# Denominators of the last attention pass from matmuls with ones, read in PSUM

## The chip, the cores and the metric

The kernel runs on one core of a Trainium2 chip. The metric is the device time of one execution in microseconds (us): the median of seven runs before the change is 894.89 us (894.72 to 896.04). One further execution was recorded by the hardware profiler; all durations below come from it. Its engines are TensorE (PE for matmuls, PEld for weight loads), VectorE (DVE), ScalarE (ACT), GpSimd (POOL) and SyncE (SP, which issues the DMAs here). Matmul results go to PSUM, which has eight banks of 512 fp32 columns; everything else on the chip is kept in SBUF.

## The reference

Two identical transformer layers over 2048 tokens of width 448, with the same weights: attention with 16 heads of 28 columns, and a feed-forward part of width 1792 with a squared ReLU. Cut to what matters:

```
def _A_ref(x, wqkv, wo):
    qkv = (x @ wqkv).reshape(B, S, 3, H, Dh)      # H = 16, Dh = 28
    scores = einsum("bhqd,bhkd->bhqk", q, k) * Dh ** -0.5
    p = softmax(scores, axis=-1)
    o = einsum("bhqk,bhkd->bhqd", p, v)
    return o.reshape(B, S, D) @ wo
def _B_ref(x, w1, b1, w2, b2):
    h = maximum(x @ w1 + b1, 0)
    return (h * h) @ w2 + b2
for _ in range(2):
    x = x + _A_ref(_layernorm(x), A_wqkv, A_wo)
    x = x + _B_ref(_layernorm(x), B_w1, B_b1, B_w2, B_b2)
return x
```

## The kernel before

**Tiles and passes.** Tokens lie in 16 tiles of 128 (`tb` 0 to 15). Heads are padded from 28 to 32 rows and worked on four at a time, a head group `g` of 0 to 3, so one group fills the 128 partitions with four strips `hh` of 32. Queries are cut into blocks `qb`: of two tiles, but of one tile each for the last two blocks of layer 1 (tile 14 and tile 15). A pass is one block and one head group over all keys. The last pass of the list (`end`, number 115) is layer 1, tile 15, head group 3; the last four passes are the four head groups of tile 15.

**Scores, exponentials, products.** `s_stream` writes scores in groups of three units of 512 columns into one of two three-bank PSUM buffers (`sc`, L809); a unit is one head strip, so consecutive matmuls sit in different 32-row strips of TensorE. To keep TensorE busy it may write the same scores again (`again`, L800), if its own clock says that there is room. ScalarE takes the exponential of each group (`pt`, L834); a few units are exponentiated on VectorE instead. `p_stream` multiplies the probabilities with the values (L982): the matmuls of one pass accumulate into one bank `oT`, each head in a column strip of 32 (`tile_position=(0, 32*hh)`), in the order strip 0, 1, 2, 3, 0, 1, ... V is padded with ones in its columns 28 to 31, so the rows 28 to 31 of each strip of `oT` hold the sum of the probabilities: the softmax denominator. In a pass of tile 15 there are 64 such matmuls of 128 columns, in four steps of 16 (one step for every four key tiles `kb`); a step of the last pass is issued as soon as its exponentials exist.

**Normalising.** When a pass is done, VectorE copies `oT` to `oT_sb` in SBUF (L1005). For most blocks the denominators go through DRAM and are inverted there in pairs (`norm_pair`). For tile 15 `norm_stream` does it on the engines: a fp32 matmul with the selection matrix `sel` spreads each head's denominator over its 32 rows in a bank `den` (L1047), VectorE inverts that bank (L1053) and multiplies (L1058) into `oTn`.

**What follows.** `chain` then runs for each block: the product with `wo` (L553 `wo,oTn`, four matmuls, one per head group; for tile 15 each waits for its own group), the sum with x on VectorE (L1113), the statistics (L448, L449), the inverse root on GpSimd (L470, L471), the normalisation (L520), transposes on TensorE (L493), their copy (L505), 14 slices of `w1` with four matmuls of 128 columns each (56, L553 `w,xnT`), ReLU (L1158 on ScalarE, L1160 on VectorE), square (L1165, L1167), the product with `w2` (one matmul for the bias and 14 more, 448 columns; for tile 15 in two parts of 320 and 128 columns, `HALF`), the sum with x and the store of the tile (L1188, on SP's queue).

**What sets the order.** Nothing is scheduled by hand or by a compiler: `Planner` runs all these streams against a cost model of its own and emits each engine's instructions in that order. Each operation names what it depends on, what buffer it acquires and what it releases. A PSUM bank (`bank`) comes from two single-bank pools (the page calls tiles there `mt`, `oT`, `den`, `tp`) and, once all scores are issued (`s_left` empty, token `"send"`), also from the two score buffers, whose tiles the page then calls `sc`. A matmul tile holds its bank until VectorE or ScalarE has read it.

Of the kernel before, what the change touches and what calls it, by code (L numbers as in the profile page):

```python
# [11 lines left out]
DT = mybir.dt  # L12
AF = mybir.ActivationFunctionType
ALU = mybir.AluOpType
P = 128
H = 16
DH = 28
DHP = 32
G = 4
QB = 512  # L20
QR = 256
# [196 lines left out]
def kernel(  # L218
# [12 lines left out]
    nc = tc.nc  # L231
# [29 lines left out]
    pl = Planner()  # L261
# [144 lines left out]
    def bank(o, name):  # L406

        if o.res in R_m:
            return ps_m[R_m.index(o.res)].tile([P, 512], DT.float32, name=name, tag="m")[:, :]
        return ps_sc.tile([P, 3 * 512], DT.float32, name="sc", tag="sc")[:, 0:512]  # L410
# [260 lines left out]
    for pi, (l, qb, g, kbs, first, last) in enumerate(passes):  # L671
        r = 4 // blocks[l][qb][1]
# [259 lines left out]
    def p_stream():  # L932


        for pi, (l, qb, g, kbs, first, last) in enumerate(passes):
            nt = blocks[l][qb][1]
            r, n = 4 // nt, nt * P
            todo = list(kbs[::r])
            end = pi == len(passes) - 1
            some = 1 if end else CHUNK  # L940
            hold = todo[0 if end else min((HOLD if nt == 2 else HOLD1) * len(todo) // 8, len(todo) - 1)]
            box = {}
            p_next[0] = next(i for i, u in enumerate(units) if u[0] == pi and u[1] == hold) + G - 1

            def done(kb):

                return ("u", pi, kb) in pl.tok and all(("x" if k == 3 else "e", gi) in pl.tok for gi, k, _ in where[pi, kb])

            def got(kb):

                yield Op("-", 0.0, None, deps=[("u", pi, kb)])
                yield Op("-", 0.0, None, deps=[("e", gi) for gi, k, _ in where[pi, kb] if k < 3])
            yield from got(hold)
            while todo:
                now = [kb for kb in todo if done(kb)][:some]
                if len(now) < min(some, len(todo)):
                    kb = next(kb for kb in todo if not done(kb))
                    if ("u", pi, kb) not in pl.tok or any(k < 3 and ("e", gi) not in pl.tok for gi, k, _ in where[pi, kb]):
                        yield from got(kb)
                        continue  # L960
                    if (e_now[1] - min(gi for gi, _, _ in where[pi, kb]) < NPT - KEEP and e_now[1] < len(gbuf) - 1
                            and len(todo) > len(now) + 1):
                        yield Op("-", 0.0, None, deps=[("e", e_now[1] + 1)])
                        continue

                    now = sorted(now[:some - 1] + [kb])
                    yield Op("-", 0.0, None, deps=[("x", gi) for gi, k, _ in where[pi, kb] if k == 3])
                todo = [kb for kb in todo if kb not in now]
                begin, close = "t" not in box, not todo

                def fn(e, now=now, begin=begin, close=close, box=box, pi=pi, l=l, g=g, r=r, n=n):
                    if "t" not in box:
                        p_next[0] = None
                        box["t"] = bank(box["o"], "oT")
                    held[0] -= sum(k == 3 for kb in now for _, k, _ in where[pi, kb])
                    for kb in now:
                        for i in range(r):
                            for gi, k, hh in where[pi, kb]:
                                p, c0 = gbuf[gi]["pt"], k * 512 + i * n
                                if k == 3:  # L980
                                    p, c0 = gbuf[gi]["pd"], i * n
                                nc.tensor.matmul(box["t"][DHP * hh:DHP * hh + DHP, 0:n],  # L982
                                                 lhsT=V_sb[l][:, kb + i, 4 * g + hh, :],
                                                 rhs=p[:, c0:c0 + n],
                                                 start=begin and kb == now[0] and i == 0,
                                                 stop=close and kb == now[-1] and i == r - 1,
                                                 tile_position=(0, DHP * hh))
                by = [(("x" if k == 3 else "e"), gi) for kb in now for gi, k, _ in where[pi, kb]]
                o = Op("PE", 0.02 + 0.22 * len(now), fn,
                       deps=[*by, *{("V", l, kb + i) for kb in now for i in range(r)}],  # L990
                       acq=None if "o" in box else pools_now(),
                       rel=[gbuf[gi][w] for w, gi in by], mode="col")
                box.setdefault("o", o)
                yield o
            res = {}
            def ev(e, box=box, first=first, last=last, g=g, res=res, n=n, l=l, qb=qb):
                pair = pairs.get((l, qb, g // 2))
                src = box["t"][:, 0:n]
                if last:
                    dst = res["t"] = pair["t"][:, g % 2, :]  # L1000
                    dst = dst[:, 0:n]
                else:
                    dst = part(l, qb, g)
                if first:
                    nc.vector.tensor_copy(out=dst, in_=src)  # L1005
                else:
                    nc.vector.tensor_tensor(out=dst, in0=src, in1=part(l, qb, g), op=ALU.add)
            if last and (l, qb, g // 2) not in pairs:
                def both(e, l=l, qb=qb, g=g):
                    pairs[l, qb, g // 2]["t"] = osp.tile([P, 2, QR], DT.float32, name="oT_sb")  # L1010
                pairs[l, qb, g // 2] = {"own": Op("DVE", 0.0, both, acq=R_os), "ev": [], "res": []}
                yield pairs[l, qb, g // 2]["own"]
            pair = pairs[l, qb, g // 2] if last else None
            oe = Op("DVE", 0.15 + n / 930, ev, deps=[o], rel=box["o"])
            yield oe
            if last:
                pair["ev"].append(oe)
                pair["res"].append((g, res))
                if qb == len(blocks[l]) - 1:
                    pl.spawn(3, norm_stream(l, qb, g, res, oe, pair))  # L1020
                elif len(pair["ev"]) == 2:
                    pl.spawn(3, norm_pair(l, qb, g - g % 2, pair))

    def norm_start(l, qb):
        if (l, qb) not in oTn_of:
            def take(e):
                oTn_of[l, qb][0] = np_.tile([P, G, QR], DT.bfloat16, name="oTn")
            oTn_of[l, qb] = [None, Op("DVE", 0.0, take, acq=R_on)]
            yield oTn_of[l, qb][1]

    def norm_end(l, qb, m, gs):

        norm_done.setdefault((l, qb), []).extend([m] * gs)
        if len(norm_done[l, qb]) == G - ((l, qb) == (1, len(blocks[1]) - 1)):
            pl.spawn(LASTP if (l, qb) == (1, len(blocks[1]) - 1) else NLP + 0.1 * (qb - len(blocks[1])) if l == 1 and qb >= len(blocks[1]) - NL else 4 + 0.1 * qb, chain(l, qb))

    def norm_stream(l, qb, g, res, oe, pair):


        t0, nt = blocks[l][qb]  # L1040
        n = nt * P
        box = {}
        yield from norm_start(l, qb)

        def den(e):
            box["t"] = bank(d, "den")
            nc.tensor.matmul(box["t"][:, 0:n], lhsT=sel[:, :], rhs=res["t"][:, 0:n], start=True, stop=True)  # L1047
        d = Op("PE", 0.1 + n * 4 / 2400, den, deps=[oe], acq=pools_now())
        yield d

        def rcp(e):
            box["r"] = rp.tile([P, 2, QR], DT.float32, name="rec")[:, 0, :]
            nc.vector.reciprocal(out=box["r"][:, 0:n], in_=box["t"][:, 0:n])  # L1053
        r = Op("DVE", n * 0.0066, rcp, deps=[d], rel=d, acq=R_rec)
        yield r

        def mul(e):
            nc.vector.tensor_tensor(out=oTn_of[l, qb][0][:, g, 0:n], in0=res["t"][:, 0:n],  # L1058
                                    in1=box["r"][:, 0:n], op=ALU.mult)
        m = Op("DVE", 0.13 + n / 930, mul, deps=[r, oTn_of[l, qb][1]], sets=("on", l, qb, g))  # L1060
        yield m
        yield Op("DVE", 0.0, None, deps=[m], rel=r)
        pair.setdefault("mul", []).append(m)
        if len(pair["mul"]) == 2:
            yield Op("DVE", 0.0, None, deps=[m], rel=pair["own"])
        norm_end(l, qb, m, 1)

    def norm_pair(l, qb, g, pair):
# [200 lines left out]
```

The softmax here doesn't subtract the row's maximum and nothing guards it: scores larger than these inputs give would overflow.

## Time and profile before

| what | value |
|---|---|
| median of 7 runs | 894.89 us (894.72 to 896.04) |
| the profiled execution | 894.89 us |
| its span, first to last instruction | 893.1 us |
| busy: PE / DVE / ACT | 831.1 (93%) / 794.1 (89%) / 878.7 us (98%) |
| the exponentials (L834) | 683, 863.8 us |
| end of the last exponential | 877.07 us |
| last sum with x on VectorE | 890.49 to 890.78 us |
| granted TensorE clock | 1.00 in every stretch from 867.5 us to the end |

The 1.8 us between the time and the span lie outside of what the profiler records of the instructions. The page says of each group of instructions how long it was busy and what its engine waited for. The chain of waits follows the work that ended last back to the start. A timeline row is `start, duration, engine, line, operation, out<-in, shape, count`. A row of several matmuls lasts from the start of the first to the end of the last, and since they are pipelined, the step from one to the next is shorter than the duration of one: the 64 products of a pass of tile 15 last 1.08 us, and one alone some 0.22 us.

From its start to about 870 us the chain is the stream of exponentials on ScalarE. The change concerns the 23 us after that: the last pass, the normalisation of tile 15 and the feed-forward part of the tiles 14 and 15, of which the attention half of tile 14 is already done.

### The profile page before, as it was taken

The page shows a single profiled execution, that of the slowest core. Times are in us where ns is not written, and L with a number is a line of the kernel's source. Part 1 is how long each engine was busy: PE and PEld are TensorE (multiplying, and loading weights), DVE is VectorE, ACT ScalarE, POOL GpSimd, SP SyncE. Part 2 cuts the span into 40 slices and gives each one's busy share as a digit, 9 for nine tenths or more (in the row PEclk, how much of TensorE's full clock was granted, in tenths as well). Part 3 has the DMA queues.
Part 4 walks back from the last instruction along what each step waited for, and adds up shares of the span by engine and source line. Part 5 has one row for each costly group of instructions (what it writes and reads, how often), then busy time and mean ns, then how long its engine had stood idle before and what let it go on. Part 6 is the DMA issues. An engine that isn't in the chain of part 4 may idle for free.

```text
span 893.1 us, 29098 instructions
## 1 busy us (share of the span) xinstructions
PE 831.1 (93%) x12829; PEld 458.5 (51%) x12829; DVE 794.1 (89%) x1572; ACT 878.7 (98%) x707; POOL 38.9 (4%) x98
## 2 busy tenths in 40 slices
PE   8999999998999999999989998888999999999998
PEld 4555654554545545454554554444544544545566
DVE  7988999999889999999989999899898999989654
ACT  8999999999999999999999999999999999999995
POOL 3100000000000000100000000001000000000000
PEclk9999999999999999999999999999999999999999
DMA  9100100000000000000000000011000000000100
GB/s 263 37 3 3 27 18 11 14 14 15 14 2 15 15 14 14 13 10 7 2 2 2 2 2 2 3 39 39 10 18 19 20 25 19 20 8 19 32 14 18
DMA packets 33915, 18.43 MB, mean 21 GB/s; under 512 B 18874, under 2 KB 33339, under 8 KB 33788
## 3 DMA queue, kind: packets, MB, share of 16 engines
q1 hardware_dynamic: 33788, 16.58, 6.6%
q8 instruction: 100, 1.64, 0.8%
q14 instruction: 27, 0.22, 0.1%
HBM read 14.26 MB, written 2.07 MB: 18 GB/s over the span
## 4 chain that ended last, share of the span: by engine, by line
ACT 68%; issue 12%; PE 10%; DVE 6%; DMA 2%; SPq 1%; POOL 0%; DVEq 0%
ACT pt L834 68%; PE mt L553 3%; PE sc L809 3%; PE oT L982 2%; DVE v_h L909 1%; DVE K_sb L909 1%; DMA dn<-oT_sb 1%; DMA rec<-scr 1%; DVE r L1160 1%; PE sc L553 1%; DVE st L448 1%; DVE oTn L1104 0%; SPq L303 0%; DMA x_sb<-in_A_x_dram 0%; DVE v_e L904 0%
## 5 line engine op out<-in xcount | busy, mean ns | idle before, releaser
L834 ACT ACTIVATE pt<-sc 128x1536 bf16<-128x1536 f32 (+1 forms) x683 | 863.8, 1569 | 1.8 <-PE sc L809 1.4
L809 PE MATMUL sc<-Q_sb,K_sb 32*128 32x256 bf16 (+1 forms) x5848 | 324.9, 265 | 53.9 <-ACT pt L834 47.6
L809 PEld LDWEIGHTS <-K_sb 32*128 32x128 bf16 x5848 | 157.6, 92 | 230.0 <-issue 201.3
L982 PE MATMUL oT<-pt,V_sb 128*32 128x256 bf16 (+1 forms) x4094 | 151.9, 268 | 0.6 <-DVE xnT L505 0.3
L553 PE MATMUL mt<-xnT,w 128*128 128x256 bf16 (+1 forms) x928 | 120.6, 269 | 1.1 <-DVE r L1160 0.8
L982 PEld LDWEIGHTS <-V_sb 128*32 128x32 bf16 x4352 | 91.6, 96 | 46.5 <-issue 43.3
L909 DVE SCALAR_TENSOR_TENSOR K_sb<-K_sb 128x512 f32<-128x512 uint16 x165 | 113.3, 687 | 0.9 <-PE mt L553 0.2
L909 DVE SCALAR_TENSOR_TENSOR v_h<-v_h,v_i 128x512 f32<-128x512 f32 x144 | 98.5, 684 | 0.6
L553 PEld LDWEIGHTS <-w 128*128 128x128 bf16 x952 | 78.6, 98 | 35.7 <-issue 27.5
L1160 DVE TENSOR_SCALAR r<-mt 128x512 bf16<-128x512 f32 x106 | 72.5, 684 | 14.8 <-PE mt L553 14.5
L553 PE MATMUL mt<-w,V_sb 128*128 128x448 bf16 (+2 forms) x288 | 67.6, 345 | 0.0
L892 DVE TENSOR_SCALAR v_i<-sc 128x512 int32<-128x512 f32 x72 | 49.4, 686 | 9.7 <-PE sc L809 9.3
L1113 DVE TENSOR_TENSOR x_sb<-x_sb,mt 128x448 bf16<-128x448 bf16 (+2 forms) x63 | 37.9, 606 | 13.4 <-PE mt L553 13.4
L909 DVE SCALAR_TENSOR_TENSOR v_h<-v_i 128x512 f32<-128x512 uint16 x72 | 49.2, 684 | 0.5
L470 POOL TENSOR_TENSOR ve<-mv,eps_t 128x2 f32<-128x2 f32 (+1 forms) x34 | 8.8, 259 | 840.4 <-DVE mv L449 840.4
L1218 PE MATMUL mt<-xn,ident 128*128 128x448 bf16 x130 | 43.5, 357 | 0.5 <-DVE x_sb L1113 0.3
L892 DVE TENSOR_SCALAR K_sb<-sc 128x512 int32<-128x512 f32 x55 | 37.7, 685 | 4.5 <-PE sc L809 4.3
L448 DVE BATCH_NORM_STATS2 st<-x_sb 128x6 f32<-128x448 bf16 x64 | 39.5, 617 | 1.7 <-DMA x_sb<-in_A_x_dram 1.4
L553 PEld LDWEIGHTS <-V_sb 128*128 128x128 bf16 x302 | 24.8, 98 | 25.5 <-issue 11.2
L915 DVE SCALAR_TENSOR_TENSOR V_sb<-v_h,v_e 128x512 bf16<-128x512 f32 x46 | 31.4, 684 | 0.3
L1167 DVE TENSOR_TENSOR V_sb<-r 128x512 bf16<-128x512 bf16 (+1 forms) x69 | 28.9, 420 | 2.1 <-ACT r L1158 1.5
L904 DVE TENSOR_SCALAR v_e<-v_i 128x512 int16<-128x512 int16 x72 | 30.2, 420 | 0.0
(106 smaller groups left out, 735.2 us busy)
## 6 DMA issues: line engine op xcount, KB each, us to landing
rec<-scr SPq DMA_DIRECT2D x56, 128.0 KB
x_sb<-in_A_x_dram SPq DMA_DIRECT2D x8, 224.0 KB
out_dram<-x_sb SPq DMA_DIRECT2D x15, 112.0 KB
w<-in_B_w_dram SPq DMA_DIRECT2D x1, 1568.0 KB
w<-in_B_w_dram SPq DMA_DIRECT2D x1, 1344.0 KB
dn<-oT_sb SPq DMA_DIRECT2D x56, 4.0 KB
V_sb<-in_A_wqkv_dram SPq DMA_DIRECT2D x4, 168.0 KB
scr<-dn SPq DMA_DIRECT2D x28, 8.0 KB
```

The source lines that it names most:

```text
L448: nc.vector.bn_stats(out=st[:, :], in_=x_sb[:, t0 + j, :])
L553: nc.tensor.matmul(box["t"][:, c0:c0 + n], lhsT=lhsT() if callable(lhsT) else lhsT, rhs=rhs, start=a, stop=b)
L809: nc.tensor.matmul(dst[k][:, i * nt * P:(i + 1) * nt * P], lhsT=K_sb[l][rows, g, (kb + i) * P:(kb + i + 1) * P], rhs=Q_sb[rows, g, t0 * P: ...
L834: t = nc.scalar.activation(out=pt[:, 0:n], in_=gbuf[gi]["sc"][:, 0:n], func=AF.Exp, scale=float(np.log(2.0)) * 2.0 ** -FRAC)
L892: t = nc.vector.tensor_scalar(out=box["i"], in0=two(src), scalar1=EXP_BIAS, scalar2=EXP_LOW, op0=ALU.add, op1=ALU.max)
L904: nc.vector.tensor_scalar(out=box["e"], in0=box["n"], scalar1=128.0, scalar2=128.0 * EXP_FIELD, op0=ALU.mult, op1=ALU.add)
L909: nc.vector.scalar_tensor_tensor(out=box["h"], in0=box["f"] if begin else box["h"], scalar=b, in1=box["f"], op0=ALU.add, op1=ALU.mult)
L915: nc.vector.scalar_tensor_tensor(out=box["two"](pd), in0=box["h"], scalar=b0, in1=box["e"].bitcast(DT.bfloat16), op0=ALU.add, op1=ALU.mult)
L982: nc.tensor.matmul(box["t"][DHP * hh:DHP * hh + DHP, 0:n], lhsT=V_sb[l][:, kb + i, 4 * g + hh, :], rhs=p[:, c0:c0 + n], start=begin and kb ...
L1113: nc.vector.tensor_tensor(out=x_sb[:, tb, lo:hi], in0=x_sb[:, tb, lo:hi], in1=t[:, 0:hi - lo], op=ALU.add)
L1160: nc.vector.tensor_scalar(out=r[:, 0:w], in0=t[:, 0:w], scalar1=0.0, scalar2=None, op0=ALU.max)
L1218: nc.tensor.matmul(t[:, 0:D], lhsT=ident[:, :], rhs=xns[0][:, 0:D], start=True, stop=True)
```

## The change

In the last pass every product with V (L982) is followed by a second matmul of the same probabilities with a matrix of ones (128x32, already there), into a second bank, `box["d"]`, at the same column strip. That bank then holds each head's denominator in all 32 rows of its strip. It is acquired by an operation of its own that depends on `"send"`, the last score group, and that stands ahead of the whole pass. In place of the copy to SBUF, the matmul with `sel`, the reciprocal and the product, `norm_last` has the reciprocal read the new bank and the product read `oT` in PSUM. The other three head groups of tile 15 keep `norm_stream`.

```diff
@@ p_stream
             yield from got(hold)
+            if end:
+                def den(e, box=box):
+                    box["d"] = bank(box["od"], "oT")
+                box["od"] = Op("PE", 0.0, den, deps=["send"], acq=pools_now)
+                yield box["od"]
             while todo:
...
                                                  tile_position=(0, DHP * hh))
+                                if end:
+                                    nc.tensor.matmul(box["d"][DHP * hh:DHP * hh + DHP, 0:n],
+                                                     lhsT=ones[:, :], rhs=p[:, c0:c0 + n],
+                                                     start=begin and kb == now[0] and i == 0,
+                                                     stop=close and kb == now[-1] and i == r - 1,
+                                                     tile_position=(0, DHP * hh))
...
-                o = Op("PE", 0.02 + 0.22 * len(now), fn,
+                o = Op("PE", 0.02 + (0.44 if end else 0.22) * len(now), fn,
...
                 yield o
+            if end:
+                pl.spawn(3, norm_last(l, qb, g, box, o))
+                return
@@ norm_stream
-        if len(pair["mul"]) == 2:
+        if len(pair["mul"]) == 2 or (l, qb, g) == (1, len(blocks[1]) - 1, G - 2):
             yield Op("DVE", 0.0, None, deps=[m], rel=pair["own"])
@@ new
+    def norm_last(l, qb, g, sums, o):
+        n = blocks[l][qb][1] * P
+        box = {}
+        yield from norm_start(l, qb)
+        def rcp(e):
+            box["r"] = rp.tile([P, 2, QR], DT.float32, name="rec")[:, 0, :]
+            nc.vector.reciprocal(out=box["r"][:, 0:n], in_=sums["d"][:, 0:n])
+        r = Op("DVE", n * 0.0066, rcp, deps=[o], acq=R_rec, rel=sums["od"])
+        yield r
+        def mul(e):
+            nc.vector.tensor_tensor(out=oTn_of[l, qb][0][:, g, 0:n], in0=sums["t"][:, 0:n],
+                                    in1=box["r"][:, 0:n], op=ALU.mult)
+        m = Op("DVE", 0.13 + n / 930, mul, deps=[r, oTn_of[l, qb][1]], rel=sums["o"], sets=("on", l, qb, g))
+        yield m
+        yield Op("DVE", 0.0, None, deps=[m], rel=r)
+        norm_end(l, qb, m, 1)
```

Since the planner orders everything anew, the instructions around the pass move too. Up to the products of the pass before the last (the 64 at 871.16 us) all engines have the same instructions in the same order. After that TensorE has, before and after the change:

| before | after |
|---|---|
| 12 scores, the last pass's first 16 products, `sel` | 12 scores, `sel` |
| 12 scores, 16 products, 4 transposes (tile 14) | 36 scores (12 written three times), 1 filler (L1218), 4 transposes |
| 16 scores (8 written twice) | 24 scores (8 written three times) |
| 6 `w1`, 16 products, 3 `wo`, 16 products | 64 products and 64 with ones, alternating; 3 `wo` |
| 10 `w1`, `sel`, 22 `w1`, 1 `wo` | 12 `w1`, 1 `wo` |
| 18 `w1`, 12 `w2` of 448 columns | 44 `w1` |
| 4 transposes (tile 15) | 4 transposes |
| 3 `w2` of 448 columns, 56 `w1` | 6 `w2` of 448 columns, 56 `w1`, 8 `w2` of 448 columns |
| 15 `w2` of 320 columns, 15 of 128 | 15 `w2` of 320 columns, 15 of 128, 1 `w2` of 448 |

On VectorE, between the statistics of tile 15 and its normalisation, stand two ReLUs of 512 columns where there was one of 256, and the last three sums with x come in the order 320 columns, 128 columns (tile 15), 448 columns (tile 14); before, the 448 came first. SP stores in the same order.

More of the change, by code (lines that the diff above doesn't have):

```diff
@@ L969, in p_stream, with fn @@
                 begin, close = "t" not in box, not todo
-                def fn(e, now=now, begin=begin, close=close, box=box, pi=pi, l=l, g=g, r=r, n=n):
+                def fn(e, now=now, begin=begin, close=close, box=box, pi=pi, l=l, g=g, r=r, n=n, end=end):
                     if "t" not in box:
```

## The prediction, made before the changed kernel ran

> **What bounds the kernel now.** I read the page's chain of waits first: which engine sets the end?
>
> ```profile
> ACT 68%; issue 12%; PE 10%; DVE 6%; DMA 2%; SPq 1%; POOL 0%; DVEq 0%
> ```
>
> ScalarE's exponentials do, for nearly the whole span. The change reorders nothing before 872 us, so the chain's last stretch, in order of time (start, length, what), matters alone:
>
> ```profile
> 874.99 0.55 PE sc L809 x16
> ...
> 877.26 0.34 PE oT L982 x16
> 877.60 0.66 PE mt L553 x10
> 878.26 0.29 PE sc L1047 x2
> ...
> 878.58 0.97 DVE rec L1053
> ...
> 879.57 0.30 DVE oTn L1058
> ...
> 881.28 2.27 PE sc L553 x12
> 883.55 0.22 PE sc L493 x4
> 883.78 0.57 PE sc L553 x3
> 884.34 1.89 PE mt L553 x32
> 886.24 1.34 PE sc L553 x24
> 887.58 2.89 PE mt L553 x30
> ```
>
> First a latency chain: last scores, last products, `sel`, reciprocal, product, `wo`. Then TensorE, back to back. The stretches say whether it is really full there (per engine: busy us, instructions):
>
> ```profile
> 884.30:890.50 6.20, 6.15 (x87) 5.41 (x85) 2.93 (x8) 1.79 (x3) 0.00 (x0) 1.00 0.08 22
> ```
>
> 6.15 of 6.20 us. So the end answers to what TensorE has left once tile 15's transposes (883.55) are done, and what is late from there on is late at the end. Before them it fills the wait for the statistics with `w2` of tile 14, and the timeline of TensorE shows the price of that filling:
>
> ```profile
> 881.31 2.24 PE L553 MATMUL sc<-w,V_sb 128*128 128x448 bf16 x11
> ```
>
> A lone one lasts 0.35 us, so the step is (2.24 - 0.35)/10 = 0.19 us.
>
> **The change part by part**, each shift against the profiled execution.
>
> (1) *Scores.* A filler (448 columns, 0.19) and eight more scores stand ahead of the last exponential. The 16 scores of this shape at 874.93 take 0.62 us, one 0.22, so a step is 0.40/15 = 0.027; eight cost 0.22. Sum +0.41: the last exponential (877.07 at its end; ScalarE was already waiting for these scores) ends at 877.48. The 24 scores added to the group before cost 24 x 0.018 = 0.43 (12 scores take 0.40, one 0.21) and delay that exponential, 1.33 us apart from the last, by less than the last one moves anyway.
>
> (2) *Products and ones.* What do 128 matmuls cost whose neighbours sit in pairs in the same column strip? No row before has that order in column strips. Lower bound: strips run side by side whatever the order, the step of the 64 products at 871.16 us (1.08 us, one 0.22) being 0.86/63 = 0.0137. Upper bound of an orderly queue: a strip's second matmul holds up all behind it. One strip needs 0.056 per 128 columns (22 `w1` in 1.39 us: (1.39 - 0.22)/21), plus 0.004 to start the next: 0.060 a pair. The nearest row is in row strips: three units of the scores at 269.24 us sit, by the unit list, in strips 3, 1, 3, so that two same-strip matmuls are adjacent. TensorE's timeline over the stretch 269.30 to 269.42 shows
>
> ```profile
> 269.24 0.39 PE L809 MATMUL sc<-Q_sb,K_sb 32*128 32x256 bf16 x4
> ```
>
> and the whole group, with an ordinary one behind it:
>
> ```profile
> 269.24 0.61 PE L809 MATMUL sc<-Q_sb,K_sb 32*128 32x256 bf16 x6
> ...
> 270.83 0.39 PE L809 MATMUL sc<-Q_sb,K_sb 32*128 32x256 bf16 x6
> ```
>
> Same-strip matmuls do queue up: four of them in strip 3 make 0.61 us of 0.39. But four of the six have started by 269.42. In strict order it would be three (3, 1, and the second 3), since the fourth is again strip 3 and starts only with the third's end; the one for strip 1 behind it has passed it. I take side by side, 0.0137, and keep 0.060 for a rival. The scores end at 875.55 + 0.41 = 875.96, and a run of products starts 0.07 before the end of the scores ahead of it (872.57, 872.50): from 875.89 on, the 96 matmuls that need no last exponential take 1.32, to about 877.2, and are done before it. The last 32 start 0.12 after it, as the last 16 did (877.07, 877.19): 877.60, and end 31 x 0.0137 + 0.22 = 0.65 later, 878.25, against 877.60: **+0.65**.
>
> The Trainium skill, "TensorE: Matmul & The Clock Gate", "The mechanism", speaks against this: matmuls are strictly first in, first out, only weight loads are pulled ahead. By it each ones-matmul blocks the next strip, and the sum would be the rival's, 899.4. The row at 269.42 with its four started matmuls does not agree with the rule, but it is about row strips.
>
> (3) *Removed.* Copy and `sel` stood between the last product and the reciprocal: 878.58 - 877.60 = 0.98. Only the hop from TensorE to VectorE remains, 0.05 (877.60 to the copy at 877.65): **-0.93**. Reciprocal (0.96) and product (0.29) keep their size: both read 128 fp32 columns, the first from PSUM before too; for the product from PSUM the nearest row is the copy from there, 0.29 as well. Bounds 0.25 to 0.35. Sum so far -0.28: `wo`'s fourth at 879.64. TensorE is free by then: after the pairs 3 x 0.19 + 12 x 0.056 = 1.24, from 878.1 to 879.35. The 32 products that lay in gaps under the exponentials are in (2).
>
> (4) *VectorE ahead of the normalisation.* Sum and statistics move by -0.28; the aggregate ends at 881.54, the inverse root at 882.45 in place of 882.73. But VectorE's queue now has two ReLUs of 512 columns (0.69 each) ahead of the normalisation: 881.46 + 1.38 + 0.02 = 882.86, where it began at 882.76 behind GpSimd: **+0.10** (their inputs, 4 + 32 `w1` after `wo`, are there at 882.1). Transposes depend on it, 883.32, and TensorE is idle about 0.9 us before them, all its 44 `w1` being done by 882.3. Before, they started at 883.39, late behind `w2`. The next matmul starts at 883.55 against 883.61: **-0.06**.
>
> (5) *TensorE after the transposes.* Both banks of the single pools are held by `oT` and its sums until VectorE has read them, so `w1` of tile 14 started late, and 12 `w2` that filled the statistics now come after: 11 ahead of the 128-column matmuls, 11 x 0.19 = **+2.07**, and one behind. TensorE no longer waits for tile 15's `xnT`, a gap from 884.17 to 884.29: **-0.12**. The last 128-column matmul ends 890.45 - 0.06 + 2.07 - 0.12 = 892.34.
>
> (6) *The end.* The sum of 128 columns follows (0.29, to 892.67), then that of 448 columns (0.62, to 893.3): before, the end was at 890.78. **+2.52**. The last store is then 112 KB, not 32 KB. Bounds: nothing, and 0.6 us, since 80 KB landed 1.6 us after its issue at 890.17, 32 KB after 1.45, and the 112 KB of 885.03 had packets until 2.1. I take **+0.25**. SP's queue has nothing else behind it but the end.
>
> Sum **+2.8** on a span of 893.1, whose own time is the median, 894.89: **897.7**. Its own range: with a free store (-0.25) and the 0.41 of (1) absorbed 897.0; with the store at 0.6 (+0.35) and 0.020 for each of the pairs' matmuls (127 x 0.020 + 0.22 from 875.89, +0.4) 898.4.
>
> **The rivals.** *Pairs in strict order*: 63 x 0.060 + 0.056 + 0.22 = 4.06 from 875.89, so the last ends at 879.95 and the reciprocal moves by +1.42, `wo` to 881.34, the normalisation behind the ReLUs to 883.16 + 1.40 = 884.56, the next matmul after the transposes to 885.24, +1.63 in place of -0.06: 899.4. For it: four same-strip scores took their turns; against: the passed one. If weight loads block too, a pair costs 0.112 and the end is 3.3 later; I give that 0.03.
>
> *The moved `w2` finds idle TensorE* (the other side: not slower): if the tail waited for ReLU and square of tile 15, 12 `w2` would fit in, and only (4) and (6) without its 2.07 remained: -0.06 + 0.33 + 0.25 = +0.5, 895.4. It decides from 2.2 us of idle TensorE after 884.3 on; the stretch shows 0.05. Against it then; it could also turn to a gain if the store costs nothing and the chain gives its whole -0.28.
>
> *The change doesn't do what it says*: the emitted instructions show 64 matmuls with ones and both reads of PSUM, and no second `sel`. I give it nothing.
>
> **How the numbers follow.** Forecast 0.70, strict order 0.17, blocked loads 0.03, hidden `w2` 0.07, a gain 0.03. About 0.2%, 1.8 us, is what a measurement of this kernel can tell from no change. Forecast and both slow rivals lie above 896.7: slower 0.88 (0.90 less 0.02 for what I haven't seen), same 0.07 + 0.02 = 0.09, faster 0.03. The range takes in the forecast's own and the strict order: 896.7 to 899.6.
>
> **What would show it.** Right: the row of the ones lasts 1.3 to 2.4 us with its products, the reciprocal starts near 878.3, TensorE is idle some 0.9 us before tile 15's transposes, 15 `w2` of 448 columns stand behind them, and the last instruction on VectorE is a 448-column sum near 892.7 to 893.3. A row of pairs of 3.8 us shows the strict order. Wrong altogether: TensorE idle over 1 us after the transposes.

## The result, and the profile after

| | before | after |
|---|---|---|
| median, same comparison | 895.19 us (34 runs, 893.99 to 897.79) | 897.53 us (13 runs, 896.29 to 900.52) |
| ratio | | 1.0024 [1.0015, 1.0034] |
| the profiled execution, its span | 894.89, 893.1 us | 899.53, 897.8 us |

By the ratio the changed kernel is slower by 2.15 us (1.3 to 3.0 by the interval; the ratio is the comparison's own, the two medians lie 2.34 us apart); 897.7 had been predicted. The chain of waits, shared out by engine, still puts ScalarE first:

```profile
ACT 69%; issue 12%; PE 11%; DVE 5%; DMA 2%; SPq 1%; POOL 0%; DVEq 0%
```

The two spans can't be subtracted from each other. The granted clock of the changed kernel's profiled execution, over the 40 slices of the span, has a dip in slice 28:

```profile
PEclk9999999999999999999999999998999999999999
```

Between 600 and 625 us the granted clock was 0.86 (1.00 before the change). That lies ahead of everything that the change touches: the exponentials of this execution are 0.02 us behind those of before at 519 us, and 2.66 us behind from 640 us on. The last instructions that both kernels have in the same order, the 64 products of the pass before the last, begin 2.66 us later as well (871.16 us before):

```profile
873.82 1.08 PE L987 MATMUL oT<-pt,V_sb 128*32 128x128 bf16 x64
```

So from here on every time counts from the start of those 64 products, and the **tail** is what lies between them and the end of the span. Before it is 893.11 - 871.16 = 21.95 us, after 897.75 - 873.82 = 23.93: **+1.98 us**, which agrees with the ratio. Step by step (us after the start of the 64 products; the predicted shift is the prediction's own):

| event | before | after | shift | predicted |
|---|---|---|---|---|
| last scores end | 4.39 | 4.59 | +0.20 | +0.41 |
| last exponential ends | 5.91 | 5.91 | 0 | +0.41 |
| last product or ones-matmul ends | 6.44 | 6.59 | +0.15 | +0.65 |
| reciprocal starts | 7.42 | 6.62 | -0.80 | -0.28 |
| fourth `wo` starts | 8.75 | 7.96 | -0.79 | -0.28 |
| normalisation of tile 15 starts | 11.60 | 11.05 | -0.55 | +0.10 |
| transposes of tile 15 start | 12.23 | 11.50 | -0.73 | -0.07 |
| next matmul after them starts | 12.45 | 11.73 | -0.72 | -0.06 |
| last 128-column `w2` ends | 19.29 | 20.54 | +1.25 | +1.89 |
| last sum with x ends | 19.62 | 21.41 | +1.79 | +2.52 |
| span ends (the tail) | 21.95 | 23.93 | +1.98 | +2.8 |

The table says it already: the latency chain became 0.8 us shorter, and the end came 2 us later. What TensorE does with products and ones is in its timeline:

```profile
878.35 0.25 PE L987 MATMUL oT<-pt,V_sb 128*32 128x128 bf16 x4
878.41 0.24 PE L994 MATMUL oT<-pt,ones 128*32 128x128 bf16 x4
878.47 0.24 PE L987 MATMUL oT<-pt,V_sb 128*32 128x128 bf16 x4
878.52 0.24 PE L994 MATMUL oT<-pt,ones 128*32 128x128 bf16 x4
...
880.17 0.24 PE L994 MATMUL oT<-pt,ones 128*32 128x128 bf16 x2
```

The program issues product, ones, product, ones, each pair in one column strip. The rows show four products starting together, 0.056 us later four ones, and so on: the four strips run side by side, and a matmul for a free strip passes one whose strip is taken. The fourth product of a row has passed three ones that were issued ahead of it. All 128 last from 878.35 to 880.41, 2.06 us.

What follows, on the timeline of all engines:

```profile
880.45 0.96 DVE L1090 RECIPROCAL rec<-oT 128x128 f32<-128x128 f32 x1 [2.34 <-PE oT L994]
...
881.44 0.29 DVE L1095 TENSOR_TENSOR oTn<-oT,rec 128x128 bf16<-128x128 f32 x1
...
883.61 1.35 DVE L1194 TENSOR_SCALAR r<-mt 128x512 bf16<-128x512 f32 x2
...
884.88 0.39 DVE L520 TENSOR_SCALAR xn<-x_sb,mv,rstd 128x448 bf16<-128x448 bf16 x1
...
885.32 0.40 PE L493 MATMUL sc<-ident,xn 128*128 128x128 bf16 x4 [0.71 <-DVE xn L520]
885.55 0.35 PE L553 MATMUL mt<-b2w,one 128*128 128x448 bf16 x1
885.74 1.11 PE L553 MATMUL mt<-w,V_sb 128*128 128x448 bf16 x5
...
889.81 1.68 PE L553 MATMUL mt<-w,V_sb 128*128 128x448 bf16 x8
...
893.42 0.94 PE L553 MATMUL sc<-w,V_sb 128*128 128x128 bf16 x14
...
894.20 0.35 PE L553 MATMUL mt<-w,V_sb 128*128 128x448 bf16 x1
894.40 0.29 DVE L1147 TENSOR_TENSOR x_sb<-x_sb,sc 128x128 bf16<-128x128 bf16 x1 [0.35 <-PE sc L553]
894.61 0.62 DVE L1147 TENSOR_TENSOR x_sb<-x_sb,mt 128x448 bf16<-128x448 bf16 x1
```

Reciprocal and product cost what they cost before. At 885.32 TensorE has waited 0.71 us for the normalisation (the number in brackets), where before it was writing `w2` of tile 14. Those `w2` now stand behind the transposes (885.55, 885.74, 889.81), and the last is the last matmul of all, with a sum of 0.62 us behind it in place of one of 0.29. In windows (us, busy time of PE, PEld, DVE, ACT, POOL, clock, share of the DMA engines, GB/s) the same idle time, and none after it:

```profile
884.30:890.50 6.20, 5.49 (x76) 4.47 (x74) 2.72 (x7) 3.62 (x7) 0.29 (x1) 1.00 0.01 4
890.50:894.00 3.50, 3.50 (x33) 2.49 (x31) 0.91 (x3) 0.00 (x0) 0.00 (x0) 1.00 0.00 0
```

### The profile page after: what moved, and what is told of

Same layout as the page of the kernel before. It is cut to its first block, busy times and chain, and to the rows that moved or that the text cites. A ratio compares the mean times of both kernels' runs of the same rounds, so it can differ in the third digit from the quotient of the medians.

```text
span 897.8 us, 29287 instructions
## 1 busy us (share of the span) xinstructions
PE 834.0 (93%) x12924; PEld 460.0 (51%) x12924; DVE 794.6 (89%) x1572; ACT 878.2 (98%) x706; POOL 38.9 (4%) x98
## 4 chain that ended last, share of the span: by engine, by line
ACT 69%; issue 12%; PE 11%; DVE 5%; DMA 2%; SPq 1%; POOL 0%; DVEq 0%
ACT pt L834 69%; PE sc L809 4%; PE mt L553 3%; PE oT L987 2%; PE sc L553 1%; DVE r L1194 1%; DVE v_h L909 1%; DMA rec<-scr 1%; PE mt L1252 1%; DVE K_sb L909 1%; DVE st L448 0%; SPq L303 0%; DMA x_sb<-in_A_x_dram 0%; DMA dn<-oT_sb 0%; DVE oTn L1138 0%
## 5 line engine op out<-in xcount | busy, mean ns | idle before, releaser
L553 PE MATMUL mt<-xnT,w 128*128 128x256 bf16 (+1 forms) x896 | 118.4, 271 | 0.8 <-DVE r L1194 0.5
L553 PE MATMUL mt<-w,V_sb 128*128 128x448 bf16 x274 | 67.8, 355 | 0.0
L1147 DVE TENSOR_TENSOR x_sb<-x_sb,mt 128x448 bf16<-128x448 bf16 x62 | 37.8, 614 | 12.1 <-PE mt L553 11.9
```

The source lines that it names most:

```text
L553: nc.tensor.matmul(box["t"][:, c0:c0 + n], lhsT=lhsT() if callable(lhsT) else lhsT, rhs=rhs, start=a, stop=b)
L1147: nc.vector.tensor_tensor(out=x_sb[:, tb, lo:hi], in0=x_sb[:, tb, lo:hi], in1=t[:, 0:hi - lo], op=ALU.add)
```

## The experiments

The theory that they were to test: the tail is bound by TensorE's work, and the loss comes from the order that the planner then gives that work, not from the ones themselves. Rivals: the issue order of the pairs, the wait of the whole pass for the last scores, and the two banks held. Except for the last three, each is one profile, so its tail is compared. Two pairs give the repeatability: one kernel profiled in two executions had 22.23 and 22.22, and the changed kernel and its variant with the matmuls in batches both had 23.93. (Some expectations take 23.98 for the changed kernel's tail; by the trace it is 23.93.)

**The wait alone (`e1_hold`).** The kernel before, with the last pass held back until the last scores are issued:

```diff
             yield from got(hold)
+            if end:
+                yield Op("-", 0.0, None, deps=["send"])
```

> The kernel before, with one edit: the last pass waits for the last score group before its first product, as the change makes it do; no ones, copy and sel kept. Measured by the tail: from the first of the 64 products of the pass before the last (871.16 before, 873.82 after) to the span's end, 21.94 us before and 23.98 after. The planner emits nearly the order of before (12 w2 of 448 columns ahead of tile 15's transposes, the 448-column sum not last). My theory (the loss comes from TensorE's work in a tail that it bounds, and from the w2 and the 448-column sum that come late): the waiting alone costs the 32 products that left the gaps under the exponentials (32 x 0.014 = 0.44) and nothing else, tail 22.3 to 22.6. Rival (the hold is the loss): 23.4 or more.

Measured: tail 22.34 us, +0.39 to before. The chain of waits shows how (start, length, what):

```profile
877.47 0.78 PE oT L984 x48
878.25 0.67 PE sc L553 x3
878.92 0.34 PE oT L984 x16
...
879.93 0.29 PE sc L1049 x2
880.24 0.97 DVE rec L1055
...
892.16 0.29 DVE x_sb L1115
```

Products that filled gaps under the exponentials now form one run of 48, with `wo` behind, and the last 16 find TensorE busy: they start 6.42 us after the 64 products (878.85 on the timeline) where before they started at 6.03. So the wait is a cost, but a fifth of the +1.98.

**A quarter of the ones (`e2_ones16`).** The ones only for the first four key tiles of the last pass:

```diff
-                                if end:
+                                if end and kb == 0:
...
-                                                     stop=close and kb == now[-1] and i == r - 1,
+                                                     stop=i == r - 1,
```

> The changed kernel with the same order, but matmuls with ones only for the first four key tiles: 16 in place of 64, so the denominators leave out three quarters of the keys. Rival (the 48 matmuls are paid for one by one): 48 x 0.0137 = 0.66 less, tail 23.3. My theory: in this order the first 96 of the 128 matmuls only fill the wait for the last exponential, of the ones only the last step's 16 (0.22) stand behind it, tail 23.75 to 23.9, and the later instructions shift by as much.

Measured: last product 6.36 after 6.59, so 48 ones cost 0.23 us there, but the tail is 23.49, 0.44 less, between the two numbers expected. The timeline of VectorE shows a side effect that the expectation had not seen:

```profile
876.24 0.96 DVE L1090 RECIPROCAL rec<-oT 128x128 f32<-128x128 f32 x1 [0.95 <-PE oT L994]
...
877.41 0.29 DVE L1095 TENSOR_TENSOR oTn<-oT,rec 128x128 bf16<-128x128 f32 x1 [0.21 <-PE oT L987]
```

The reciprocal depends on the ones only, so it runs ahead of the last products and the product with it waits for those alone. That gives the chain 0.42 us at `wo` (7.54 after 7.96), and TensorE's idle time before the transposes moves with it. The run prices the ones, and says less of the tail than was meant. Even so, 1.54 us of the +1.98 remain with most of the ones gone and the chain shorter still.

**Products as before, the ones behind in an operation of their own (`e3_late`).** The bank for the sums is taken late, the pass no longer waits for `"send"`:

```diff
-            if end:
-                def den(e, box=box):
...
+                if end:
+                    pend.append((now[0], by))
...
+                    while pend and "send" in pl.tok:
+                        kb, by = pend.pop(0)
...
+                        o = Op("PE", 0.24, total, deps=[*by, "send"], acq=None if "od" in box else pools_now(),
+                               rel=[gbuf[gi][w] for w, gi in by], mode="col")
```

> The changed kernel with the products of the last pass let go again as soon as their exponentials exist, and the 64 matmuls with ones in a run of their own behind the last product; their bank is taken only then, so 6 w1 of tile 14 find a bank early, as before the change. Rival (the two banks held make w1 and with it w2 late): the tail falls well below 23.98, to 23.0 or less. My theory: the run of ones (64 x 0.0137 + 0.2 = 1.1) now stands between the last product and the reciprocal, which moves back to about where it was before the change; 11 w2 of 448 columns are still emitted behind the transposes and the 448-column sum last, so the tail is longer than after, 24.3 to 24.8.

Measured: 23.71 us, outside of what either theory said. My own number took the ones for one run behind the last product; but 48 of them are issued ahead of the last 16 products, and the last matmul of the pass ends at 6.58, where it ended at 6.59. The rival's number fails for a reason that teaches more: although the bank for the sums was taken late, and the first six `w1` stand where they stood before the change, `w2` of tile 14 still stood behind the transposes. TensorE's timeline:

```profile
875.13 0.50 PE L553 MATMUL mt<-xnT,w 128*128 128x128 bf16 x6
...
882.06 0.40 PE L493 MATMUL sc<-ident,xn 128*128 128x128 bf16 x4 [1.03 <-DVE xn L520]
882.29 0.35 PE L553 MATMUL sc<-b2w,one 128*128 128x448 bf16 x1
```

So the second bank, held early, is not what moves it. The first, `oT`, is still held until the product here; `e5_fill` below holds both as the change does and bears on that.

**Eight deep in one strip (`e4_strips`).** The 128 matmuls strip by strip instead of round the strips:

```diff
-                        for i in range(r):
-                            for gi, k, hh in where[pi, kb]:
...
+                            for gi, k, hh in where[pi, kb]:
+                                for i in range(r):
+                                    prod(i, gi, k, hh, False)
+                                    prod(i, gi, k, hh, True)
```

> The changed kernel with the 32 matmuls of each step ordered strip by strip: product, ones, product, ones, ... eight in the same column strip, then the next strip. The profile after showed the pairs starting four abreast every 0.056 us, products and ones in turn, so a waiting matmul lets others pass. If it lets them pass eight deep, the 128 matmuls take the same 2.06 us and the tail is 23.98. If only a neighbour is passed, two to four strips run at a time less: the run takes 3 to 7.2 us (128 x 0.056) and the tail grows by 1 to 5 us.

Measured: 26.08 us, +2.15 to the change; the last matmul of the pass ends at 8.74 instead of 6.59. TensorE's timeline:

```profile
876.64 0.23 PE L987 MATMUL oT<-pt,V_sb 128*32 128x128 bf16 x1
876.71 0.22 PE L987 MATMUL oT<-pt,ones 128*32 128x128 bf16 x1
876.77 0.22 PE L987 MATMUL oT<-pt,V_sb 128*32 128x128 bf16 x1
876.82 0.22 PE L987 MATMUL oT<-pt,ones 128*32 128x128 bf16 x1
876.88 0.24 PE L987 MATMUL oT<-pt,V_sb 128*32 128x128 bf16 x2
876.93 0.24 PE L987 MATMUL oT<-pt,ones 128*32 128x128 bf16 x2
```

Two strips at a time, not four: the 128 last 4.2 us. One strip alone would take 128 x 0.056 = 7.2. The rows also show how far a matmul passes others. The first four of the run of eight start alone, and the first of the next strip starts together with the fifth (876.88): by then the sixth, seventh and eighth still wait, and it passes those three. At 876.82, with four still waiting, it had not started. In the changed kernel a product never has to pass more than three ones, so its order costs nothing; that of `e4` is dear.

**Products and ones in batches of four (`e8_batched`).** The opposite, so that no neighbours share a strip:

```diff
+                            for two in (False, True) if end else (False,):
+                                for gi, k, hh in where[pi, kb]:
+                                    prod(i, gi, k, hh, two)
```

> The changed kernel with four products first, one for each column strip, then four matmuls with ones, in place of pairs in one strip. If a waiting matmul lets the other strips pass, as the profile after shows it, nothing changes: the run of 128 lasts 2.06 us, tail 23.98 within 0.05. If pairs cost anything, the run is shorter and so is the tail.

Measured: tail 23.93 us, last ones-matmul 6.59, reciprocal 6.62, the same to the hundredth as with the pairs. The pairs cost nothing.

**The order alone (`e5_fill`).** The changed kernel with two dependences more: the transposes of tile 15 wait for the first `w2` of tile 14, and `w2` of tile 15 waits for the last of them.

```diff
-            t = Op("PE", 0.07 * NDC * len(xs), tr, deps=[x[1] for x in xs],
+            t = Op("PE", 0.07 * NDC * len(xs), tr, deps=[x[1] for x in xs] + ([("w2_14", 4)] if last_tile and 4 >= 0 else []),
...
+                      sets=[(mark, m) for m in range(i, k)] + ([(mark, "all")] if k == len(mms) else []) if mark else ())
...
+                    add_to_x(tb, lo, hi), 0.15 + (hi - lo) / 950, [*([] if own_deps else [hacts[-1][2]]), *([("w2_14", "all")] if end else []), ("w2",), ("b2",)],
```

> The changed kernel with the order mended by two dependences: tile 15's transposes wait for the first 6 w2 of tile 14, and tile 15's w2 for the last of tile 14. So the idle 0.71 us of TensorE ahead of those transposes is filled, and the 448-column sum and store are no longer last. Rival (the order of the w2 is the whole loss, and with it mended the shorter chain shows): tail 21.9 (as before the change) or less. My theory (TensorE bounds this tail, and its added work, 64 matmuls with ones and the products that left the gaps, stays whatever the order): 23.98 less 0.71 idle, less 0.35 for a 128-column sum in place of the 448-column one, less 0.24 for the smaller store: 22.5 to 22.9, still above the 21.95 of before.

Measured: tail **22.49** us, 1.44 less than the change, with the same ones, the same wait, the same reads from PSUM. TensorE's timeline:

```profile
881.38 0.35 PE L553 MATMUL sc<-b2w,one 128*128 128x448 bf16 x1
881.57 1.11 PE L553 MATMUL sc<-w,V_sb 128*128 128x448 bf16 x5
882.51 0.39 PE L493 MATMUL tp<-ident,xn 128*128 128x128 bf16 x4
882.74 1.30 PE L553 MATMUL sc<-w,V_sb 128*128 128x448 bf16 x6
...
889.66 0.94 PE L553 MATMUL mt<-w,V_sb 128*128 128x128 bf16 x14
```

That is the low end of what I had said, and not the rival's 21.9. Six `w2` now fill the wait for the statistics, and the row of 128 columns is the last. They stand there with both banks held as in the change, so the holding does not keep `w2` from that place. The transposes start 0.25 later for it (11.75 after 11.50), and the last 128-column matmul still ends 0.69 sooner (19.85 after 20.54); the rest of the gain, 0.75, is the 448-column matmul, sum and store that no longer end the kernel.

**Both mended (`e6_late_fill`).** The same two dependences on the kernel of `e3_late`:

> The kernel of e3 (products let go early, tail 23.71 there) with the same two dependences. My theory: less 0.7, 0.35 and 0.24 as in e5, tail 22.2 to 22.6: with the products back in the gaps the ones alone (64 x 0.0137 = 0.88, less 0.25 for the sel matmul that is gone) keep it above the 21.95 of before. Rival (order and hold are the whole loss): 21.9 or less, and then this is a version that beats both.

Measured: 22.23 us, 0.26 less than `e5_fill`, where the pass waits for the last scores, and 0.28 more than before. TensorE's timeline shows 48 ones ahead of the last products, and six `w2` (one with the bias) ahead of the transposes:

```profile
875.92 0.87 PE L1013 MATMUL sc<-pt,ones 128*32 128x128 bf16 x48
876.59 0.46 PE L984 MATMUL oT<-pt,V_sb 128*32 128x128 bf16 x16
876.84 0.44 PE L1013 MATMUL sc<-pt,ones 128*32 128x128 bf16 x16
...
880.96 1.11 PE L553 MATMUL sc<-w,V_sb 128*128 128x448 bf16 x5
881.97 0.40 PE L493 MATMUL sc<-ident,xn 128*128 128x128 bf16 x4
...
889.33 0.94 PE L553 MATMUL mt<-w,V_sb 128*128 128x128 bf16 x14
```

The number is in the range that I had given. The reason that I gave was that the ones alone keep it above the kernel before; the chain of waits shows another for most of it (start, length, what):

```profile
886.57 0.02 issue
886.59 0.61 ACT r L1207
887.20 0.04 issue
887.24 3.05 PE mt L553 x30
```

The `w2` of 320 columns, first of the 30, needs a bank that a ReLU on ScalarE is still reading. It starts at 887.24, 0.40 us after the matmul of 448 columns ahead of it (886.84), where a step is 0.19: TensorE stands still for 0.21 us, behind the transposes, by this order and not for the ones.

**Is the tail really TensorE's (`e7_nobias`)?** The kernel before without the bias matmuls of `w2` in tiles 14 and 15:

```diff
-                    [(0, hi - lo, [(one0[:, :], b2w[:, lo:hi])]
+                    [(0, hi - lo, ([] if own_deps else [(one0[:, :], b2w[:, lo:hi])])
```

> The kernel before without the three bias matmuls of the w2 products of the tiles 14 and 15 (448, 320 and 128 columns), all else in the same order; these two tiles leave out b2. If TensorE bounds the tail from tile 15's w1 on, the 320- and 128-column ones are saved there (0.136 + 0.056 = 0.19), while the 448-column one only lay ahead of w1, which waited for xnT until 884.29 in any case: tail 21.95 - 0.19 = 21.75. If TensorE doesn't bound it: 21.95. If every matmul of the tail counts: 21.95 - 0.38 = 21.57.

Measured: tail 21.76 us, -0.19; the last matmul ends at 19.10 where it ended at 19.29. That is what the two of 320 and 128 columns last behind the transposes; the one of 448, ahead of them, is free. So the two matmuls taken away behind the transposes count in full at the end, and reciprocal (7.41 after 7.42) and normalisation (11.60 both) did not move.

**Can the mended kernel beat the one before (`e9`, `e10`, `e11`)?** `e9` is `e6_late_fill` timed. `e10` (on the kernel before) and `e11` (on `e6_late_fill`) take the bias matmuls of tiles 14 and 15 away, and let GpSimd add the bias to x, ahead of time:

```diff
+            pl.spawn(EV, iter([Op("POOL", 0.8, lambda e: nc.gpsimd.tensor_tensor(
+                out=x_sb[:, t0, :], in0=x_sb[:, t0, :], in1=b2a[:, :], op=ALU.add), deps=[*ends, ("b2a",)])]))
```

> The kernel of e6 again, timed against the one before. Its tail in e6 was 22.23 against 21.95. If the tail is all that differs, the ratio is 1 + 0.28/895 = 1.0003, no change that can be measured, where the changed kernel had 1.0024. If the loss sat elsewhere (the clock, the code), the ratio stays near 1.002.

> The kernel before, its bias b2 for the tiles 14 and 15 added by GpSimd to x behind the normalisation in place of three matmuls (448, 320 and 128 columns); b2 is spread over the partitions by one DMA into keys of layer 0 that are no longer used. Complete and correct. By the TensorE bound: tail as in e7, 21.76, a ratio of 0.9998, too little to be told from no change by the times. If GpSimd's add (128x448) is late, the last sum with x waits and the tail is above 21.95.

> The kernel of e6 with the same bias on GpSimd. There TensorE was without a gap from the last products on, so all three matmuls should count: 22.23 - 0.38 = 21.85, just below the 21.95 of before and above e10. If the shortened chain decided, it would be below e10.

| | tail, us | median, us | before, us | ratio |
|---|---|---|---|---|
| `e9` | 22.22 | 894.99 | 894.79 | 1.0003 [0.9994, 1.0012] |
| `e10` | 21.87 | 894.62 | 894.79 | 0.9995 [0.9986, 1.0003] |
| `e11` | 21.76 | 895.03 | 894.79 | 0.9996 [0.9984, 1.0008] |

The ratios are again the comparison's own and not quotients of the medians.

GpSimd's additions, from its timeline in `e10`, lie well ahead of the sums that need them (1.03 us each):

```profile
873.97 1.03 POOL L1138 TENSOR_TENSOR x_sb<-x_sb,K_sb 128x448 bf16<-128x448 bf16 x1 [1.43 <-DVE xn L522]
...
882.58 1.03 POOL L1138 TENSOR_TENSOR x_sb<-x_sb,K_sb 128x448 bf16<-128x448 bf16 x1 [0.51 <-DVE xn L522]
```

Mending the order and the wait takes the whole measurable loss back: the interval of `e9` lies below that of the change (1.0015 to 1.0034) and holds 1. None of the three is shown to beat the kernel before; tails 0.08 and 0.19 us shorter are below what can be timed.

In `e10` the last matmul ends 0.18 us sooner (19.11 after 19.29) and the last sum with it, but the tail is only 0.08 shorter. The other 0.11 us lie between the last packet of the last store and the engines' closing instructions, 0.92 us in `e10` and `e11` and 0.81 before and in `e6`; why the end takes longer with the additions on GpSimd stays open.

`e11` missed its expectation: 21.76 and not 21.85, and below `e10`, not above. TensorE was not without a gap in `e6`, as the expectation had it. In `e11` the 320 columns go to a score bank and don't wait; the last matmul ends at 18.99 where it ended at 19.58 in `e6`, 0.59 sooner, of which the three matmuls are 0.38 and that wait 0.21. So with the three bias matmuls gone from both, the kernel with the ones ends its last matmul 0.11 us ahead of the one without (18.99 and 19.11): they don't make the tail longer there.

## Why the prediction was right, and where it was off

The direction and the path held: a shorter latency chain, then idle time, then a longer run of TensorE. The +1.98 splits by the runs into **1.44** for the order (change to `e5`), **0.26** between `e5` and `e6`, where the pass no longer waits (the wait alone was 0.39 in `e1`), and **0.28** that is left between `e6` and the kernel before. Of this last, 0.21 is the wait for ScalarE that the order of `e6` has, so that the ones, beyond the `sel` that they replace, come to less than 0.1 us. The size is too large in the prediction, and that 897.7 lies so near to 897.53 is luck in part: the kernel before came out at 895.19 beside it and not at 894.89, and the tail grew by 1.98 and not by 2.8.

(1) *Scores.* This is the **term that was mis-sized**: +0.41 for the last exponential, measured 0. The scores ended only 0.20 later. The 16 products that used to stand in front of `sel` of the head group before had left that place, so its reciprocal and, behind it on VectorE, the normalisation of tile 14 came 0.20 earlier (2.01 and 2.88 after 2.21 and 3.08), and that paid for the filler; the eight scores were left. And even their 0.20 was absorbed. The timeline of ScalarE, before,

```profile
872.87 4.20 ACT L834 ACTIVATE pt<-sc 128x1536 bf16<-128x1536 f32 x3
```

and after,

```profile
875.52 4.21 ACT L834 ACTIVATE pt<-sc 128x1536 bf16<-128x1536 f32 x3
```

has the last three exponentials in 4.2 us either way. The last two started 0.27 and 0.21 us late, and their records shrank from 1.957 to 1.686 and from 1.421 to 1.215 us. Exponentials start 1.33 us apart and last up to 1.95, so a part of each record lies under the one ahead, and a start that is late by less than that part moves no end. I had let the whole delay through; the low end of the forecast's own range (897.0) was built in part on this absorption.

(2) *Products and ones.* Side by side, as taken: 2.06 us for 128. The strict order is refuted by the rows of four, and `e8` puts the price of the pairs at nothing. The end of the last, +0.15 for the predicted +0.65, is less by the 0.41 of (1) and by 0.09 of its own.

(3) *Removed.* 0.03 us remain of 0.98; -0.95 against -0.93. Reciprocal 0.96, product from PSUM 0.29. Right.

(4) *VectorE.* The two ReLUs do stand ahead of the normalisation and take back a part of the gain: reciprocal -0.80, normalisation -0.55. They cost 0.25 us there, not the 0.38 of the sum. Idle time before the transposes 0.71, predicted 0.9. The next matmul came 0.72 and not 0.06 earlier: of the 0.66 between, 0.52 is inherited from the reciprocal (-0.80 for -0.28), and 0.13 is what the ReLUs held up less.

(5) *TensorE behind the transposes.* From there to the end of the last 128-column matmul +1.25 + 0.72 = +1.97 us, predicted +1.95. Right in size, but **the reason given was wrong**: I put it down to the two banks held by `oT` and its sums. `e3` takes the bank for the sums late and starts `w1` 4.34 us after the 64 products, as the kernel before does (4.35), and `w2` is as late as ever; `e5` holds both banks and has six `w2` ahead of the transposes. The planner issues `w2` behind the `w1` of its tile; with a shorter chain the transposes are due before it gets there. The chain's own gain moves the work that hid its wait. That the due time alone decides this is argued from the order; shown is that the banks don't, and that naming the order does (`e5`).

(6) *The end.* From the last 128-column matmul to the end of the last sum +0.54 (predicted +0.63), the store behind it +0.19 (predicted +0.25). Right.

Summed, against the predicted +2.8: -0.66 for the start behind the transposes, which is (1) with its shares in (2) and (4), +0.02 for (5), -0.09 and -0.06 for (6): with the unrounded 2.77, +1.98.

## What to carry to other kernels

Where an engine is full behind a latency chain, a shorter chain need not be worth anything by itself (here 0.80 us of chain gave nothing): ask which work filled the wait, and where it goes when the wait is gone. When a planner or compiler orders anew, compare the order first; one matmul moved to the very end, with a wider sum and store behind it, cost 0.73 us here, nearly all that the chain had gained. And subtract two traces from the last instruction that both have in common, not span from span (here +1.98 against +4.6).

## What the hardware did that was not expected

*Matmuls pass a waiting one, to a limited depth.* 128 matmuls of 128 columns in four column strips take 2.06 us when pairs share a strip, the same when none do (`e8`), and 4.2 us, two strips abreast, when runs of eight share one (`e4`). In `e4` a matmul starts past three that wait for their strip, and not past four; other lengths of run were not tried. The Trainium skill, "TensorE: Matmul & The Clock Gate", "The mechanism", has matmuls strictly first in, first out; in column strips these runs do not agree with it.

*A late start on ScalarE need not be a late end.* Starts up to 0.27 us late left the end of the last exponential at 5.91 us, in every kernel run here.
